# Moving GpSimd's projection sums and the deviations between the two steps of a pair

## The chip, the cores and the metric

The kernel runs on one core of a Trainium2 chip. The metric is the device time of one execution in microseconds (us). A core has five engines with a queue of instructions each: TensorE (PE in the profile, its weight loads PEld), VectorE (DVE), ScalarE (ACT), GpSimd (POOL) and SyncE (SP, which here only issues transfers). They wait for each other on semaphores.

## The reference

```
X = np.fft.rfft(x, axis=1)                 # x: 8 x 3136 x 256
y = np.fft.irfft(X * (filt_r + 1j*filt_i), n=3136, axis=1)
h = y.reshape(25088, 256) @ w_in           # 256 -> 1024
e = np.exp(h - max(h)); solu = h * e / (sum(e) + 1e-9)
ln = (solu - mean(solu)) / sqrt(var(solu) + 1e-6) * g_ln
out = ln @ w_out                           # 1024 -> 256
```

A filter along the sequence in the frequency domain, for each of 8 batch elements, and then a SoLU network with a layer norm on each of the 25088 tokens. All is float32.

## The kernel before, in words

The Fourier transforms are done as products with tables, in two stages, each with a passage through DRAM. The first element is transformed before the network starts; the transforms of the other seven are laid out by a hand-written plan (`PLAN`, and lists of jobs by step) beside the network for the elements before them.

The network takes 196 blocks of 128 tokens, two blocks to a pair. A pair is worked at by two calls of `step(k)`: the even step k = 2j and the odd one k = 2j + 1. There is no scheduler: every engine runs its instructions in the order in which `step` writes them (`tc.manual_schedule()`), so a line's place in `step` is its place in the queue of its engine. Both large products are done by a scheme of seven half-size products instead of eight; for it some sums of the inputs and weights are needed. In `step`, these things concern the change:

- `product(j, m)` (L715) are the seven products of the first matrix. Their input sums come from `pair_sums(j + 1)` on GpSimd (L704), at the start of the odd step.
- `exponential`, `normalize`, `square` and `turn` make solu of a block, the sum of squares (`var`), and a VectorE transpose into `turn`.
- `regroup(p, i)` (L790, its DMAs L799) fetches the two blocks of a pair out of the turned tile with eight DMAs of SP, into tiles `solu_t`. It stands in the even step of j for pair p = j - 3.
- `project_sums(p, step)` (L818) are GpSimd's four sums for the second matrix: step 0 makes `u1` and a difference that is written over a part of `solu_t`, step 1 makes `u2` and `u4`. All four are recorded at L702, inside the helper `sum_of`.
- `project(p, m)` (L834, matmuls at L844) are the seven products of the second matrix: 1, 2, 6 and 7 in the odd step, 5, 3 and 4 in the even step after it. Products 5, 6, 7 and 3 need the four sums.
- `deviations(p)` (L802) is done once for a group of two pairs: GpSimd makes `rs`, one over the standard deviation, with two small instructions (L806, L808), and SP stores it to DRAM (`rows`, L810). `regroup_deviations(g)` (L812) reloads it with four DMAs of SP in the order of the regrouped tokens (`rs_t`, L816).
- `keep_out` (ScalarE, L856) and `finish_out` (VectorE, L860) scale the projection by `rs_t`; `store_out` (SP, L868) writes it.
- For the transforms, GpSimd adds two quarters of the input (L260) before PE's products at L269, and issues the DMAs `t<-d` (`fetch_back`, L356), `d<-x` (L280), `d<-g` (L343) and `f<-f_dram` (L642). SP loads the input of these transforms (`x<-in_x_dram`, L245).

The jobs lists `stores[k]`, `products[k]` and `top[k]` run at the start of a step, `late[k]` and `loads[k]` at its end. `u2` and `u4` have one buffer each, the other sums and `solu_t` two.

Of the kernel before, what the change touches and what calls it, by code (L numbers as in the profile page):

```python
# [94 lines left out]
def kernel(  # L95
# [88 lines left out]
    class Spectrum:  # L184
# [114 lines left out]
        def product(self, i, out, lhsT, rhs):  # L299
            for v in range(self.units[i][1]):  # L300
                nc.tensor.matmul(out=out[:, v, :], lhsT=lhsT(v), rhs=rhs[:, v, :],  # L301
                                 start=True, stop=True)
# [398 lines left out]
    def sum_of(out, in0, in1, op):  # L701
        nc.gpsimd.tensor_tensor(out=out, in0=in0, in1=in1, op=op)  # L702

    def pair_sums(j):  # L704

        s14 = upool.tile([P, 2, P], FP32, name=f"s14_{j}", tag="s14")
        s23 = wk.tile([P, 2, P], FP32, name=f"s23_{j}", tag="s23")
        sums[j] = s1, s2, s3, s4 = s14[:, 0, :], s23[:, 0, :], s23[:, 1, :], s14[:, 1, :]
        a11, a12, a21, a22 = (tokens(2 * j + i, c) for i in range(2) for c in range(KD))
        sum_of(s1, a21, a22, ALU.add)  # L710
        sum_of(s2, s1, a11, ALU.subtract)
        sum_of(s3, a11, a21, ALU.subtract)
        sum_of(s4, a12, s2, ALU.subtract)
# [15 lines left out]
    def keep(j, k, i):  # L729

        if k not in hs:
            hs[k] = hpool.tile([P, DFF], FP32, name=f"h_{k}", tag=f"h{k % 2}")
        nc.scalar.copy(out=h_half(k, i), in_=ms[j, 0])  # L733
# [17 lines left out]
    def exponential(k):  # L751

        e = wk.tile([P, DFF], FP32, name="e", tag="e")
        esum = small.tile([P, 1], FP32, name="esum", tag="esum", bufs=2)
        nc.scalar.activation(out=e, in_=hs[k], func=AFT.Exp, bias=nmaxs.pop(k)[:, 1:2], scale=-1.0,  # L755
                             accum_out=esum)
        es[k] = e, esum
# [44 lines left out]
    def deviations(p):  # L802
        g, second = divmod(p, 2)
        if not second:
            rs = small.tile([P, 4], FP32, name=f"rs_{g}", tag="rs", bufs=2)
            nc.gpsimd.tensor_scalar(out=rs, in0=variances.pop(g), scalar1=1.0 / DFF, scalar2=EPS_LN,  # L806
                                    op0=ALU.mult, op1=ALU.add)
            nc.gpsimd.tensor_tensor(out=rs, in0=rs, in1=neg_half, op=ALU.pow)  # L808
            rs_rows[g] = rows = rs_dram.tile([P, 4], FP32, name=f"rows_{g}", tag="rows")
            nc.sync.dma_start(out=rows, in_=rs)  # L810

    def regroup_deviations(g):  # L812
        rows = rs_rows.pop(g).rearrange("(a p) b -> b p a", p=32)
        rss[g] = small.tile([P, 4], FP32, name=f"rs_t_{g}", tag="rs_t")
        for b in range(4):
            nc.sync.dma_start(out=rss[g][32 * b:32 * b + 32, :], in_=rows[b])  # L816

    def project_sums(p, step):  # L818

        (a11, a12), (a21, a22) = solu_ts[p, 0], solu_ts[p, 1]  # L820
        if step == 0:
            s1 = upool.tile([P, KF // 2, P], FP32, name=f"u1_{p}", tag="u1")
            sum_of(s1, a21, a22, ALU.add)
            sum_of(a21, a11, a21, ALU.subtract)
            solu_sums[p] = s1, None, a21, None
        else:
            s2 = spool.tile([P, KF // 2, P], FP32, name=f"u2_{p}", tag="u2")
            s4 = spool.tile([P, KF // 2, P], FP32, name=f"u4_{p}", tag="u4")
            s1, _, s3, _ = solu_sums[p]
            sum_of(s2, s1, a11, ALU.subtract)  # L830
            sum_of(s4, a12, s2, ALU.subtract)
            solu_sums[p] = s1, s2, s3, s4

    def project(p, m):  # L834

        bank = {1: 0, 6: 0, 5: 0, 3: 0, 2: 1, 7: 1, 4: 1}[m]
        if m in (1, 2):
            pos[p, bank] = ps_o.tile([P, DFF // 2], FP32, name=f"o{m}_{p}", tag=f"o{bank}")[:, 0:P]
        s1, s2, s3, s4 = solu_sums[p]
        lhs = {1: solu_ts[p, 0][0], 2: solu_ts[p, 0][1], 4: solu_ts[p, 1][1], 5: s1, 6: s2, 7: s3,  # L840
               3: s4}[m]
        w = w_out_sb[:, {1: 0, 2: 1, 3: 2, 5: 3, 6: 4, 7: 5, 4: 6}[m]]
        for f in range(KF // 2):
            nc.tensor.matmul(out=pos[p, bank], lhsT=lhs[:, f, :], rhs=w[:, f, :],  # L844
                             start=f == 0 and m in (1, 2, 7), stop=True, skip_group_check=True)
# [8 lines left out]
    def keep_out(p, i, to):  # L854
        rs = out_half(p, i, 0)[1]
        nc.scalar.activation(out=out_half(p, *to)[0], in_=pos[p, 0], func=AFT.Copy, scale=rs)  # L856
# [89 lines left out]
    pairs = blocks // 2  # L946

    def step(k):
        j, odd = divmod(k, 2)
        p = j - (LAG - 1) // 2 if odd else j - (LAG + 1) // 2  # L950
        if not 0 <= p < pairs:
            p = None
        hid, proj = k < blocks, p is not None
        for job in top[k] + stores[k] + products[k]:
            job()
        if odd and j + 1 < pairs:
            pair_sums(j + 1)
        if not odd:
            if hid:
                product(j, 1)  # L960
                keep(j, k, 0)
            if 2 <= k < blocks + 2:
                exponential(k - 2)
            if proj:
                project(p, 5)
                keep_out(p, 1, (0, 1))
            if hid:
                product(j, 2)
            if 3 <= k < blocks + 3:
                turn(k - 3)  # L970
            if hid:
                finish(j, k, 0, (k, 0), 1)
            if proj:
                finish_out(p, 1, 1, (0, 1), 1)
            for job in early[k]:
                job()
            if 3 <= k < blocks + 3:
                square(k - 3)
            if hid:
                product(j, 6)  # L980
                keep(j, k + 1, 0)
            if proj:
                project(p, 3)
                keep_out(p, 0, (0, 1))
                project(p, 4)
            for job in spectrum_loads[k]:
                job()
            if 0 <= j - 3 < pairs:
                regroup(j - 3, 0)
                regroup(j - 3, 1)  # L990
            if 0 <= j - 4 < pairs:
                project_sums(j - 4, 1)
            if 0 <= j - 3 < pairs:
                deviations(j - 3)
            if hid:
                product(j, 7)
            if 2 <= k < blocks + 2:
                normalize(k - 2)
            for job in second_parts[k] + middle[k] + first_parts[k]:
                job()  # L1000
            if proj:
                finish_out(p, 1, 0, (1, 0), 1)
                store_out(p)
        else:
            if hid:
                product(j, 5)
                keep(j, k - 1, 1)
                finish(j, k, 1, (k - 1, 1), 2)
            for job in early[k]:
                job()  # L1010
            if proj:
                project(p, 1)
                keep_out(p, 0, (0, 0))
                project(p, 2)
                finish_out(p, 0, 0, (0, 0), 1)
            if 2 <= k < blocks + 2:
                exponential(k - 2)
            if hid:
                product(j, 3)
                product(j, 4)  # L1020
            if 0 <= j - 3 < pairs:
                project_sums(j - 3, 0)
                if (j - 3) % 2 == 0:
                    regroup_deviations((j - 3) // 2)
            if proj:
                project(p, 6)
                project(p, 7)
            for job in second_parts[k] + middle[k]:
                job()
            if 3 <= k < blocks + 3:  # L1030
                turn(k - 3)
            if hid:
                finish(j, k - 1, 1, None, 0)
                finish(j, k, 0, (k, 0), 2)
            if 2 <= k < blocks + 2:
                normalize(k - 2)
            if proj:
                keep_out(p, 1, (1, 0))
            if 3 <= k < blocks + 3:
                square(k - 3)  # L1040
            for job in first_parts[k]:
                job()
        for job in late[k] + loads[k]:
            job()
        if k in (0, 1, 3, 4, 5, 6, 7):
            prepare_w_out(k - (k > 2))
# [37 lines left out]
```

## Time and profile before

| | |
|---|---|
| median of 3 runs | 1651.52 us (1638.6 to 1654.56) |
| the profiled execution | 1631.78 us, its span 1630.0 us, granted clock 0.986 |
| PE busy | 1551.7 us, 95% of the span |
| DVE busy | 1303.8 us, 80% |
| POOL busy | 1151.2 us, 71% |
| ACT busy | 903.5 us, 55% |
| POOL's first projection sum, 98 times | 1262 / 1276 / 2315 ns (least, median, most) |
| the eight regrouping DMAs of a pair | 128 KB each, issued by SP |

Busy time is a sum over the span; an engine that is idle beside a busy PE costs nothing by that. In the lines of waits the numbers are the total in us, the number of times, and the longest.

### The profile page before, as it was taken

How to read it: one execution, taken by the hardware profiler on the slowest of the kernel's cores; microseconds unless marked ns; L12 is line 12 of the kernel's file. 1: busy time of each engine (PE TensorE's matmuls, PEld its weight loads, DVE VectorE, ACT ScalarE, POOL GpSimd, SP SyncE). 2: the span in 40 equal slices, each digit the busy share in tenths (PEclk: the TensorE clock that was granted, in tenths of full speed). 3: DMA queues.
4: the chain of work that ended last, by engine and by line, in shares of the span. 5: the costliest groups of instructions: out<-in, count | busy, mean ns of one | idle time of the engine just before them, and what ended most of it. 6: DMA issues, size and time to landing. Idle time of an engine off the chain costs nothing. (4 is left out here: it accounts for less than half of the span.)

```text
span 1630.0 us, 36971 instructions
## 1 busy us (share of the span) xinstructions
PE 1551.7 (95%) x12710; PEld 1048.3 (64%) x12710; DVE 1303.8 (80%) x2630; ACT 903.5 (55%) x1772; POOL 1151.2 (71%) x1328
## 2 busy tenths in 40 slices
PE   5898899999999999999999999999999999999997
PEld 1353366666666676667766676666766777777766
DVE  1686788898888889987889789887989777777772
ACT  2135455656655665565556655566555655566662
POOL 4446886588676867697687967778476666677774
PEclk8999899999999999999999999999999999999999
DMA  9887878777887768866787678866786555444443
GB/s 266 251 274 242 237 212 241 210 216 191 198 239 221 198 182 257 230 190 180 188 250 203 172 194 219 235 185 170 203 223 160 127 130 128 104 109 104 110 109 101
DMA packets 377805, 312.13 MB, mean 191 GB/s; under 512 B 63322, under 2 KB 343395, under 8 KB 377619
## 3 DMA queue, kind: packets, MB, share of 16 engines
q1 hardware_dynamic: 306260, 169.81, 40.8%
q0 software_dynamic: 34464, 101.68, 21.2%
q10 hardware_dynamic: 36896, 38.28, 7.9%
q8 instruction: 103, 1.69, 0.5%
q14 instruction: 82, 0.67, 0.1%
HBM read 124.86 MB, written 81.50 MB: 127 GB/s over the span
## 5 line engine op out<-in xcount | busy, mean ns | idle before, releaser
L844 PEld LDWEIGHTS o<-w_out_sb,solu_t 128*128 128x128 f32 x3136 | 382.0, 192 | 50.0 <-issue 43.6
L723 PE MATMUL m<-w_in_sb,s 128*128 128x512 f32 x784 | 398.7, 609 | 10.5 <-ACT h L733 5.3
L844 PE MATMUL o<-w_out_sb,solu_t 128*128 128x128 f32 x3136 | 401.5, 276 | 3.2 <-DVE ot L860 2.8
L844 PEld LDWEIGHTS o<-w_out_sb,u 128*128 128x128 f32 x2352 | 307.9, 192 | 147.4 <-issue 104.6
L702 POOL TENSOR_TENSOR u<-solu_t 128x512 f32<-128x512 f32 x98 | 132.5, 1352 | 276.6 <-DMA solu_t<-turn 165.8
L844 PE MATMUL o<-w_out_sb,u 128*128 128x128 f32 x2352 | 312.1, 276 | 8.7 <-ACT ot L856 7.8
L723 PE MATMUL m<-w_in_sb,y 128*128 128x512 f32 x588 | 311.1, 613 | 5.4 <-DVE nmax L747 3.3
L733 ACT COPY h<-m 128x512 f32<-128x512 f32 x294 | 173.2, 589 | 240.5 <-PE m L723 201.8
L771 DVE SCALAR_TENSOR_TENSOR h<-e,rsum,h 128x1024 f32<-128x1024 f32 x196 | 294.8, 1504 | 6.9
L856 ACT ACTIVATE ot<-o,rs_t 128x128 f32<-128x128 f32 x392 | 144.0, 367 | 254.1 <-PE o L844 238.3
L779 ACT ACTIVATE h<-h,nmu 128x1024 f32<-128x1024 f32 x196 | 224.9, 1148 | 59.6 <-DVE turn L787 59.2
L747 DVE CUSTOM_DVE_ANT_0 h<-m,h 128x512 f32<-128x512 f32 x196 | 134.0, 684 | 148.2 <-ACT h L733 94.8
L787 DVE STREAM_TRANSPOSE turn<-h 128x1024 f32<-128x1024 f32 x196 | 243.1, 1240 | 3.2
L755 ACT ACTIVATE e<-h,nmax 128x1024 f32<-128x1024 f32 x196 | 225.2, 1149 | 6.5 <-DVE h L771 6.5
L702 POOL TENSOR_TENSOR u<-solu_t,u 128x512 f32<-128x512 f32 x98 | 147.8, 1508 | 79.2 <-PE o L844 74.2
L723 PEld LDWEIGHTS m<-w_in_sb,s 128*128 128x128 f32 x784 | 128.6, 192 | 100.0 <-issue 85.6
L723 PEld LDWEIGHTS m<-w_in_sb,y 128*128 128x128 f32 x588 | 96.9, 192 | 104.4 <-issue 52.2
L860 DVE SCALAR_TENSOR_TENSOR ot<-o,rs_t,ot 128x128 f32<-128x128 f32 x294 | 102.0, 347 | 76.0 <-ACT ot L856 57.1
L702 POOL TENSOR_TENSOR u<-u,solu_t 128x512 f32<-128x512 f32 x98 | 158.9, 1621 | 1.2
L702 POOL TENSOR_TENSOR solu_t<-solu_t,solu_t 128x512 f32<-128x512 f32 x98 | 142.4, 1453 | 7.7
L702 POOL TENSOR_TENSOR s<-y 128x128 f32<-128x128 f32 x196 | 103.4, 527 | 0.4
L372 PEld LDWEIGHTS py<-wb_t,t 50*64 50x64 f32 x3584 | 57.6, 134 | 43.2 <-issue 21.2
(114 smaller groups left out, 1963.8 us busy)
## 6 DMA issues: line engine op xcount, KB each, us to landing
solu_t<-turn SPq DMA_DIRECT2D x784, 128.0 KB
out_dram<-ot SPq DMA_DIRECT2D x196, 128.0 KB
t<-d POOLq DMA_DIRECT2D x112, 200.0 KB, 4.4
d<-x POOLq DMA_DIRECT2D x100, 200.0 KB, 5.5
f<-f_dram POOLq DMA_DIRECT2D x39, 512.0 KB, 7.9
d<-g POOLq DMA_DIRECT2D x39, 512.0 KB, 5.5
t<-d ACTq DMA_DIRECT2D x36, 512.0 KB
x<-in_x_dram SPq DMA_DIRECT2D x112, 98.0 KB
```

Of the source, the lines that this page charges most:

```text
L372: nc.tensor.matmul(out=views[g][64 * h:64 * h + 64, cb, i, :], lhsT=t4[rows, i, c0:c0 + 64], rhs=wb_t[rows, 0:N1], start=True, stop=True)
L702: nc.gpsimd.tensor_tensor(out=out, in0=in0, in1=in1, op=op)
L723: nc.tensor.matmul(out=ms[j, bank], lhsT=lhsT, rhs=w_in_sb[:, w, :], start=m in (1, 2, 7), stop=True, skip_group_check=True)
L733: nc.scalar.copy(out=h_half(k, i), in_=ms[j, 0])
L747: nc.vector.tensor_tensor_reduce(out=h_half(k, i), in0=ms[j, bank], in1=h_half(*kept), scale=1.0, scalar=sofar, op0=ALU.add, op1=ALU.min, ...
L755: nc.scalar.activation(out=e, in_=hs[k], func=AFT.Exp, bias=nmaxs.pop(k)[:, 1:2], scale=-1.0, accum_out=esum)
L771: nc.vector.scalar_tensor_tensor(out=solu, in0=e, scalar=rsum, in1=solu, op0=ALU.mult, op1=ALU.mult, accum_out=nmu)
L779: nc.scalar.activation(out=solu, in_=solu, func=AFT.Square, bias=nmu, scale=-float(DFF), accum_out=variances[g][:, i:i + 1])
L787: nc.vector.transpose(out=turns[g][:, :, i, :], in_=solus[k].rearrange("p (f j) -> p f j", j=32))
L844: nc.tensor.matmul(out=pos[p, bank], lhsT=lhs[:, f, :], rhs=w[:, f, :], start=f == 0 and m in (1, 2, 7), stop=True, skip_group_check=True)
L856: nc.scalar.activation(out=out_half(p, *to)[0], in_=pos[p, 0], func=AFT.Copy, scale=rs)
L860: nc.vector.scalar_tensor_tensor(out=ot, in0=pos[p, bank], scalar=rs, in1=out_half(p, *kept)[0], op0=ALU.mult, op1=ALU.add)
```

## The change

All four sums of a pair now stand in the even step: the first two, which stood in the odd step before, at its very start, the other two where they were. The deviations' two GpSimd instructions and their store move from the even step into the odd one, after the pair sums, to where the first two sums had been. The reload of the deviations moves from the odd step to the start of the next even step. No instruction is added or removed, and no size changes.

```
         hid, proj = k < blocks, p is not None
+        if not odd and 0 <= j - 4 < pairs:
+            if j % 2 == 0:
+                regroup_deviations((j - 4) // 2)
+            project_sums(j - 4, 0)
         for job in top[k] + stores[k] + products[k]:
             job()
...
             if 0 <= j - 4 < pairs:
                 project_sums(j - 4, 1)
-            if 0 <= j - 3 < pairs:
-                deviations(j - 3)
             if hid:
                 product(j, 7)
...
             if 0 <= j - 3 < pairs:
-                project_sums(j - 3, 0)
-                if (j - 3) % 2 == 0:
-                    regroup_deviations((j - 3) // 2)
+                deviations(j - 3)
             if proj:
                 project(p, 6)
```

More of the change, by code (lines that the diff above doesn't have):

```diff
@@ L953, in step @@
         hid, proj = k < blocks, p is not None
+        if not odd and 0 <= j - 4 < pairs:
+            if j % 2 == 0:
+                regroup_deviations((j - 4) // 2)
+            project_sums(j - 4, 0)
         for job in top[k] + stores[k] + products[k]:
@@ L992, in step @@
                 project_sums(j - 4, 1)
-            if 0 <= j - 3 < pairs:
-                deviations(j - 3)
             if hid:
@@ L1021, in step @@
             if 0 <= j - 3 < pairs:
-                project_sums(j - 3, 0)
-                if (j - 3) % 2 == 0:
-                    regroup_deviations((j - 3) // 2)
+                deviations(j - 3)
             if proj:
```

## The prediction

> **What bounds the kernel now.** I read the page's busy shares first, then the windows by stage, the waits of PE and POOL, the timeline of one pair, and the chain at the end.
>
> ```profile
> PE 1551.7 (95%) x12710; PEld 1048.3 (64%) x12710; DVE 1303.8 (80%) x2630; ACT 903.5 (55%) x1772; POOL 1151.2 (71%) x1328
> 800.00:1000.00 200.00, 197.15 (x1770) 135.31 (x1769) 174.62 (x346) 117.80 (x233) 151.89 (x175) 0.99 0.77 210
> 1400.00:1500.00 100.00, 99.86 (x571) 72.05 (x570) 77.68 (x173) 61.68 (x122) 73.22 (x73) 1.00 0.43 108
> 1600.00:1630.00 30.00, 19.13 (x161) 18.12 (x159) 3.15 (x9) 4.41 (x12) 12.38 (x11) 0.93 0.38 98
> PE pa L269 <- POOL x L260: 7.2, 5, 2.0
> POOL u L702 <- DMA solu_t<-turn: 142.3, 31, 9.1
> ```
>
> The first line is the page; the next three are windows (length, then busy time of PE, PEld, DVE, ACT, POOL, then clock, DMA share, GB/s). PE is the bound: in the stage where Fourier work and the network run together (about 250 to 1250 us) it is 98 to 99% busy, from 1250 to 1580 us over 99%; only the last 30 us are loose. The last two lines are waits between 250 and 1250 us (total, times, longest). POOL waits 142.3 us for the regrouped tile and PE hardly notices; what PE loses to POOL is 7.2 us, before the forward transform, on L260, the sum of quarters. So a gain must come out of a few microseconds there or at the end, however large POOL's wait is.
>
> One pair on POOL, then PE, SP and ACT at the same place (start, duration, idle and releaser in brackets):
>
> ```profile
> 810.51 1.85 POOL L702 TENSOR_TENSOR u<-solu_t 128x512 f32<-128x512 f32 x1 [6.78 <-DMA solu_t<-turn]
> 812.44 1.27 POOL L702 TENSOR_TENSOR solu_t<-solu_t,solu_t 128x512 f32<-128x512 f32 x1
> 813.65 1.09 POOL L356 DMA_DIRECT2D t<-d  x2
> 818.93 0.51 POOL L806 TENSOR_SCALAR rs<-var 128x4 f32<-128x4 f32 x1
> 819.52 1.04 POOL L808 TENSOR_TENSOR rs<-rs,neg_half 128x4 f32<-128x4 f32 x1
> 821.38 1.28 POOL L260 TENSOR_TENSOR x<-x 113x512 f32<-113x512 f32 x1
> 822.71 0.65 PE L269 MATMUL pa<-x,wq_t 49*64 49x512 f32 x2 [2.00 <-POOL x L260]
> 820.59 0.36 SPq L810 DMA_DIRECT2D rows<-rs  x1
> 822.73 2.45 SPq L245 DMA_DIRECT2D x<-in_x_dram  x4
> 825.77 4.20 SPq L816 DMA_DIRECT2D rs_t<-rows  x4
> 830.12 7.85 SPq L799 DMA_DIRECT2D solu_t<-turn  x8
> 835.75 0.37 ACT L856 ACTIVATE ot<-o,rs_t 128x128 f32<-128x128 f32 x1 [0.30 <-PE o L844]
> ```
>
> The reader is to see that the two deviation instructions stand just ahead of the sum of quarters that PE waits for, and that ACT's first use of the reloaded deviations comes ten microseconds after the reload began. The end of the chain of waits:
>
> ```profile
> 1603.30 2.09 DMA rows<-rs
> 1606.76 2.98 DMA rs_t<-rows
> 1609.92 0.38 ACT ot L856
> 1610.43 2.93 PE o L844 x24
> ```
>
> Here nothing covers the deviations' trip through DRAM: store, reload, scaling and PE follow each other, and the end waits for them.
>
> [...]POOL stood 6.78 us before its first sum with its loads queued behind. [...]SP's reloads waited 25.8 us in all for the store of rows, so SP's place in its queue matters. [...] the same first sum takes 1.262 to 2.315 us, so moved sums may meet other VectorE work.
>
> **The change, part by part.** No instruction is added or removed, and the order on PE, ACT and DVE stays. Only POOL and SP are reordered.
>
> *The first two sums (u1, and the one written back into solu_t).* On POOL they now stand behind the odd step's tail, the loads t<-d (L356, 1.09 us for two), and in front of the same stores and second sums as before. So the wait for the regrouped tile is still in POOL's queue; "a step later" moves it past 1.09 us of issues at most. Where the tile is late, the issues are hidden in the wait; where it is ready, the sums start 1.1 us later. Cover: product 6 of the projection started 4 to 5 us after the third sum (u2), which it needs, in most pairs of this stage, later still after 1250 us. In six pairs of it the cover was 1.3 us or less (pair 39: the third sum ends at 817.5, product 6 starts at 817.7), but before each of these POOL had waited over 5 us for the tile, and there the move costs nothing. Earlier t<-d traffic (two DMAs of 200 KB) can slow the regrouping in flight: nothing to 2 us in such a pair; a loss of 1 us in a few of them is taken in the range, nothing in the sum. Another meeting with VectorE costs or saves up to 1 us (2.3 against 1.3), beside a cover of 4: nothing.
>
> *The deviations on POOL.* 818.93 to 820.53, 1.6 us in 49 of 98 pairs, move from before to after the sum of quarters and the pair sums. Both come 1.6 us earlier in these pairs. Each PE wait on L260 that the timeline shows in the stage follows a deviation, as here. Five waits of 7.2 us, the longest 2.0; with the weight load that precedes them some 8.5 us. At most 1.6 us comes back of each, and not all are that long: gain 7 us, bounds 4 and 9. What is late next there is PE's own queue.
>
> *SP.* The store of rows moves behind the stores of the output and the x loads, the four reloads to the start of the next even step, ahead of eight regroupings as before. Output and x loads lose a wait (SP waited 23.6 us for rs in all); PE shows no wait for either: gain nothing to 2, taken 0. The store now needs POOL's pair sums, then 1.6 us. Worked at the pair above: rs ends at about 825.4, where the pair sums ended, 4.8 us later than before; store lands 2.1 us later, 827.6; the reloads, 1.8 us when SP is free and 4.2 us as here, end at 829.4 to 831.9; 2.7 us to landing (1607.2 to 1609.9 at the end) gives 832.1 to 834.6. ACT needs them at 835.75, so 1.1 to 3.6 us remain. For the other groups of this stage I took the end of the pair sums and of the first projection product from the timeline: between them lie 7.1 us in the shortest, about 10 in the middle. The trip needs 6.7, up to 9.5 under load. A dozen groups would then wait up to 2.4 us, 16 us of ACT in all, if every trip were loaded. Before, ACT waited 4.2 us in four cases in this stage, and once 4.2 us at the end. PE has three products (2.6 us) before product 6 adds into the bank that the scaling reads, so short waits pass it by; as an estimate half reaches it. I take a quarter of the loaded case, 4 us of ACT, 2 us of PE; bounds 0 and 8.
>
> The regroupings of the second pair of a group wait for the reloads: 0 to 2.4 us later than before. POOL then waits that much longer, but u2 has its 4 to 5 us: nothing.
>
> *The end.* POOL's order is the same there. On SP the last store of rows follows two output stores (1.3 us) that stood behind it: 1604.4 against 1603.30. Nothing hides it: plus 1.1 us, bounds 0.5 and 2.
>
> Sum: -7 + 2 + 1.1 = about -4 us. The profiled execution was 1631.78 us (span 1630.0), so 1628 in its terms; the median of the three runs is 1651.52, and its runs lie 1638.6 to 1654.56. I put the difference on the median: 1647.5.
>
> **The rivals.**
> *The deviations arrive late (slower).* Mechanism: ACT stands before its first scaling (L856) for rs_t, and exponentials and copies of h queue behind it. For it: four output scalings in this stage already met late reloads; SP has one queue and the x loads lie ahead of the store. Against: ACT is 55% busy, and the 2.6 us of products above. It begins to cost at a trip of 7 us, at 9.5 us PE loses 8 us. With a trip of 11 us in all groups the shortfalls add up to about 40 us of ACT, half on PE, 20: less 4 of the net gain, +16, giving 1667.5. It decides from 11 us.
> *POOL's lateness ran through more than L260 shows (faster).* Earlier pair sums, t<-d and x loads would also take waits now listed under DVE and ACT (PE's listed waits in the stage are 20 us in all). All of these and none of the losses: -18, giving 1633.5. Against: most are waits for ACT and DVE, whose order is kept.
> *Nothing moves.* PE is at 98 to 99% and the few waits return in another pair: 0 to +1.1, 1652.
>
> **How the numbers follow.** Forecast, -9 to -1 us: 0.5. Nothing moves, within 3 us: 0.22. Late deviations: 0.17, of which 0.12 over 1% (16.5 us is 1%, about what a measurement can tell from no change). Faster chain: 0.11, of which 0.08 over 1%. So faster 0.08, same 0.80, slower 0.12. Range: the forecast with its bounds, and the spread of the runs, gives 1635 to 1656; reaching towards the rivals 1634 to 1662.
>
> **What would show it.** Right: PE's wait on L260 in the stage falls from 7.2 to under 2 us; POOL's wait for solu_t<-turn stays above 100 us, now behind t<-d; the second sums start within 2 us of where they stood against PE; ACT's wait on rs_t stays under 15 us; the last rows store starts about 1 us later against the last regrouping. Wrong: ACT waits of tens of microseconds for rs_t, PE waiting on POOL's u sums, or the stage from 1250 to 1580 us below 99% on PE.

## The result, and the profile after

The changed kernel takes 1704.31 us (median of four runs, 1696.06 to 1709.93). The kernel before, run on the same chip, takes 1645.86 us (1638.6 to 1654.56). The ratio is 1.0349, with a 95% interval of 1.0274 to 1.0424: slower by 58 us where the forecast was 4 us faster, and outside the range. The profiled execution took 1696.06 us with a span of 1694.2, so 64 us more span than the one before.

First the busy time of each engine in the changed kernel; then the chain of waits that ended last, by engine, of the kernel before; then the same of the changed kernel, by engine and by line:

```profile
PE 1567.6 (93%) x12710; PEld 1060.9 (63%) x12710; DVE 1290.8 (76%) x2630; ACT 904.8 (53%) x1772; POOL 1141.4 (67%) x1328
```

```profile
PE 23%; DVE 1%; SPq 0%; issue 0%; DMA 0%; ACT 0%; POOL 0%; DVEq 0%; ACTq 0%
```

```profile
PE 46%; DMA 18%; POOL 4%; DVE 3%; SPq 3%; issue 3%; ACT 1%; ACTq 0%; POOLq 0%; DVEq 0%
PE o L844 22%; PE m L723 19%; DMA solu_t<-turn 5%; DMA rows<-rs 4%; DMA rs_t<-rows 3%; DMA out_dram<-ot 2%; PE py L372 2%; DMA t<-d 2%; DMA x<-in_x_dram 1%; PE pa L269 1%; SPq L799 1%; PE pc L301 1%; POOL u L702 1%; POOL s L702 1%; DMA de<-de_tbl 1%
```

PE has fallen from 95 to 93%. In the changed kernel transfers have 18% of the chain, and the store and reload of the deviations (rows, rs_t) stand among its lines by name; before, they had 0%. The two chains are not of one length (the shares sum to about a quarter of the span before and over three quarters after), so the 18% names the lines and does not measure the loss.

The windows by stage (length, busy PE, PEld, DVE, ACT, POOL, then clock, DMA share, GB/s), first of the kernel before for the stage as a whole, then four of after:

```profile
250.00:1250.00 1000.00, 980.72 (x9031) 671.44 (x9028) 868.75 (x1716) 585.61 (x1159) 740.78 (x865) 1.00 0.76 206
```

```profile
250.00:1250.00 1000.00, 943.26 (x8507) 646.27 (x8509) 804.08 (x1619) 554.26 (x1096) 697.38 (x829) 0.98 0.73 197
800.00:1000.00 200.00, 189.78 (x1639) 130.72 (x1637) 158.79 (x321) 110.67 (x218) 143.82 (x170) 0.97 0.72 197
1460.00:1560.00 100.00, 100.00 (x574) 72.58 (x573) 78.17 (x173) 62.35 (x124) 71.80 (x74) 1.00 0.43 108
1660.00:1690.00 30.00, 20.11 (x152) 19.14 (x152) 3.16 (x9) 4.13 (x12) 12.61 (x12) 0.89 0.35 91
```

Two things are lost in the long stage: PE stands more, and its clock is 0.97 to 0.98 instead of 0.99 to 1.00, so that 943 us of busy PE do less than they look. The light stage is as full as before. Read by the start of a pair's first product, the changed kernel is 13.7 us late at pair 16 (384 us before), 59.8 at pair 76 (1306 us) and 59.1 at pair 96 (1561 us), and 64 at the end. So 14 us are lost by 384 us, about 46 between 384 and 1306, nothing in the light stage, and 5 at the end.

The waits of after between 250 and 1300 us (total, times, longest), SP's among them:

```profile
POOL u L702 <- DMA solu_t<-turn: 147.3, 28, 10.2
...
ACT ot L856 <- DMA rs_t<-rows: 62.1, 19, 8.9
...
PE o L844 <- ACT ot L856: 23.2, 12, 5.1
...
ACT h L733 <- DMA rs_t<-rows: 17.7, 4, 7.0
...
DVE diff L254 <- DMA x<-in_x_dram: 15.2, 8, 4.4
...
SPq L816 <- DMA rows<-rs: 157.1, 32, 8.0
```

The same waits of before, in the same stretch:

```profile
ACT ot L856 <- DMA rs_t<-rows: 4.3, 4, 1.8
...
PE o L844 <- ACT ot L856: 0.7, 1, 0.7
...
DVE diff L254 <- DMA x<-in_x_dram: 5.7, 5, 2.3
...
SPq L816 <- DMA rows<-rs: 23.0, 16, 5.1
```

All listed waits of PE in this stretch have grown from 18.7 to 58.9 us; 23.2 us of them are for the scaling. PE's wait on the sum of quarters (L269 on L260) has no line any more. Two waits have grown together: ScalarE stands for the deviations, and SP stands at their reload, up to 8 us in each of 32 groups.

One of the later groups, on SP, then ACT and PE:

```profile
854.39 1.32 SPq L868 DMA_DIRECT2D out_dram<-ot  x2
855.95 2.19 SPq L245 DMA_DIRECT2D x<-in_x_dram  x4
858.23 0.53 SPq L810 DMA_DIRECT2D rows<-rs  x1
866.03 2.09 SPq L816 DMA_DIRECT2D rs_t<-rows  x4
868.22 8.46 SPq L799 DMA_DIRECT2D solu_t<-turn  x8
876.78 1.31 SPq L868 DMA_DIRECT2D out_dram<-ot  x2
878.28 2.23 SPq L245 DMA_DIRECT2D x<-in_x_dram  x4
...
875.54 0.37 ACT L856 ACTIVATE ot<-o,rs_t 128x128 f32<-128x128 f32 x1 [6.91 <-DMA solu_t<-turn]
...
876.05 2.05 PE L844 MATMUL o<-w_out_sb,u 128*128 128x128 f32 x8 [4.54 <-ACT ot L856]
```

GpSimd ended rs at 857.50. SP issued the store at 858.23, behind two output stores and four x loads, and could issue the reload only at 866.03: 7.8 us, in which SP did nothing. The reloads were issued by 868.12, and ScalarE's scaling ran at 875.54, 7.4 us later. (The trace names solu_t as what ended ScalarE's wait; the scaling reads rs_t, not solu_t.) So the trip took 18.0 us from the end of rs to the scaling (13.1 in the middle of the late groups), ScalarE stood 6.9, and PE, after its three covering products, 4.5. Behind SP's hold the regrouping of the next pair, the output stores and the x loads went out late as well.

There is a second place where ScalarE stands. ScalarE issues loads of its own (ACTq), and some of them wait for the reload, on SP, ScalarE and PE:

```profile
472.12 3.00 SPq L816 DMA_DIRECT2D rs_t<-rows  x4
...
477.40 0.37 ACTq L683 DMA_DIRECT2D de<-de_tbl  x1
477.81 0.59 ACT L733 COPY h<-m 128x512 f32<-128x512 f32 x1 [6.99 <-DMA rs_t<-rows]
...
478.54 1.68 PE L723 MATMUL m<-w_in_sb,s 128*128 128x512 f32 x2 [3.73 <-ACT h L733]
```

The load of a table (L683) and the copy of h behind it read nothing of rs_t. In the trace the load waits for the semaphore that the first reload, issued at 472.12, was to raise, and goes out at 477.40, when that reload has landed (477.38). Most of the line `ACT h L733 <- DMA rs_t<-rows` above is such stops. No run tested them by themselves.

What PE's stop costs beyond itself is seen in the windows of after around it:

```profile
866.00:871.00 5.00, 5.00 (x27) 3.24 (x25) 3.29 (x7) 0.59 (x1) 4.12 (x6) 1.00 0.74 224
...
876.00:878.00 2.00, 1.95 (x9) 1.98 (x10) 1.97 (x4) 1.03 (x2) 0.00 (x0) 0.50 0.70 178
...
880.00:882.00 2.00, 2.00 (x20) 1.08 (x20) 1.93 (x6) 0.84 (x3) 1.10 (x1) 0.58 0.57 179
882.00:884.00 2.00, 2.00 (x15) 0.96 (x8) 1.51 (x3) 2.00 (x5) 0.79 (x1) 1.00 0.22 78
```

The granted clock is 1.00 ahead of the stop, 0.50 when PE goes on, and 1.00 again only from about 882: five to six microseconds at about half speed, 2.8 us lost on top of 4.5. This group is not alone: in this stage of after PE stands longer than 2 us nine times (2.4 to 5.1 us, four of them for ScalarE's scaling, three for its copies of h or t, one each for VectorE and GpSimd), and each time 1.6 to 3.0 us of clock are lost in the 6 us behind it. The stretches at 0.50 last 3.4 or 6.8 us there. Before, it never stands longer than 2.0 us there, but both stops of 2.0 us, on the sum of quarters, were followed by 3.4 us at 0.50 as well, 1.7 us lost each. One of them is the stop that the prediction shows at 822.71; this window of before lies behind it:

```profile
824.00:827.00 3.00, 3.00 (x10) 1.97 (x10) 1.03 (x1) 2.65 (x6) 2.84 (x6) 0.50 0.87 236
```

Not every such stop has a lower clock behind it: before, two of 2.4 us (from 1586.7 and 1608.0 us) were followed by 6 us at 1.00, and so was one of 2.6 us in after (from 201.4 us). What decides it is not shown.

The end of the chain of after:

```profile
1664.59 5.04 DMA rows<-rs
1669.65 0.30 SPq L816
...
1682.27 0.38 ACT ot L856
```

The last store takes 5.04 us where it took 2.09, and after the reload the chain runs over the regrouping and the output stores instead of going straight to the scaling. (This is the scaling of the last pair, 1682.27; the chain gives an output store as what it waited for.)

From the trace one can add up what PE loses over the whole run: the time between two matmuls where it is over 0.3 us, and, outside of these, the clock that was not granted (one less the share, times the length of each clock record). Both are worked out from the records of the profiled executions (the runs are those of the next section), and their change accounts for the change of the span within 7 us:

| kernel | PE stands | clock lost while it runs | sum less before | span less before |
|---|---|---|---|---|
| before | 60.4 | 18.9 | | |
| after | 109.7 | 35.7 | +66.1 | +64.2 |
| deviations only | 98.4 | 31.1 | +50.1 | +56.5 |
| older scale | 96.9 | 35.2 | +52.8 | +51.6 |
| older scale, reload last | 70.9 | 21.0 | +12.6 | +8.8 |
| reload by GpSimd | 129.4 | 40.2 | +90.2 | +90.5 |
| reload last | 409.7 | 129.4 | +459.8 | +454.9 |

### The profile page after: what moved, and what is told of

It reads as the page before. It is cut to its first block, busy times and chain, and to the rows that moved or that the text cites. A ratio compares the mean times of both kernels' runs of the same rounds, so it can differ in the third digit from the quotient of the medians.

```text
span 1694.2 us, 36993 instructions
## 1 busy us (share of the span) xinstructions
PE 1567.6 (93%) x12710; PEld 1060.9 (63%) x12710; DVE 1290.8 (76%) x2630; ACT 904.8 (53%) x1772; POOL 1141.4 (67%) x1328
## 4 chain that ended last, share of the span: by engine, by line
PE 46%; DMA 18%; POOL 4%; DVE 3%; SPq 3%; issue 3%; ACT 1%; ACTq 0%; POOLq 0%; DVEq 0%
PE o L844 22%; PE m L723 19%; DMA solu_t<-turn 5%; DMA rows<-rs 4%; DMA rs_t<-rows 3%; DMA out_dram<-ot 2%; PE py L372 2%; DMA t<-d 2%; DMA x<-in_x_dram 1%; PE pa L269 1%; SPq L799 1%; PE pc L301 1%; POOL u L702 1%; POOL s L702 1%; DMA de<-de_tbl 1%
## 5 line engine op out<-in xcount | busy, mean ns | idle before, releaser
L844 PEld LDWEIGHTS o<-w_out_sb,u 128*128 128x128 f32 x2352 | 312.3, 195 | 184.5 <-issue 134.4
L844 PEld LDWEIGHTS o<-w_out_sb,solu_t 128*128 128x128 f32 x3136 | 389.1, 195 | 47.5 <-issue 43.0
L844 PE MATMUL o<-w_out_sb,solu_t 128*128 128x128 f32 x3136 | 407.3, 279 | 2.4 <-DVE ot L860 2.3
L844 PE MATMUL o<-w_out_sb,u 128*128 128x128 f32 x2352 | 319.6, 280 | 39.8 <-ACT ot L856 34.6
L733 ACT COPY h<-m 128x512 f32<-128x512 f32 x294 | 173.3, 589 | 252.8 <-PE m L723 218.8
L771 DVE SCALAR_TENSOR_TENSOR h<-e,rsum,h 128x1024 f32<-128x1024 f32 x196 | 297.3, 1517 | 6.9
L702 POOL TENSOR_TENSOR solu_t<-solu_t,solu_t 128x512 f32<-128x512 f32 x98 | 153.5, 1566 | 7.7
L702 POOL TENSOR_TENSOR u<-u,solu_t 128x512 f32<-128x512 f32 x98 | 147.3, 1503 | 0.9
L702 POOL TENSOR_TENSOR s<-y 128x128 f32<-128x128 f32 x196 | 95.5, 487 | 0.4
```

Source lines behind the costliest of these rows:

```text
L771: nc.vector.scalar_tensor_tensor(out=solu, in0=e, scalar=rsum, in1=solu, op0=ALU.mult, op1=ALU.mult, accum_out=nmu)
```

## The experiments

The first theory was that ScalarE's wait for late deviations is the loss (A in the expectations, where a letter is used). Its rivals were that the moved sums of GpSimd are (B), or half and half (C). That SP's hold at the reload is a cause came in after the third run. All ratios are to the kernel before, run on the same chip, with 95% intervals. "Lateness" is the time from the end of a group's first projection product to its scaling, summed over the groups of 250 to 1300 us where it is over half a microsecond: 11.0 us before, 91.7 after.

**The sums alone.** Of the change only the move of the first two sums; deviations and reload as before.

```
+        if not odd and 0 <= j - 4 < pairs:
+            project_sums(j - 4, 0)
...
-                project_sums(j - 3, 0)
```

> Only the sums move: all four in the even step as in the changed kernel; deviations, their store and their reload stay where they were before. Theory A (the loss is ScalarE's wait for the reloaded deviations, whose trip through DRAM now starts some 4 us nearer to its use): the time is that of before, 1646 us, within 8; ScalarE's wait for rs_t stays below 15 us in all, against 70 in the changed kernel. Rival B (the sums' move does it: the t<-d loads, issued earlier, slow the regrouping, and the sums then hold up the projection): the time is near 1704. Rival C (half and half): about 1675.

Measured: 1634.16 us against 1640.37, ratio 0.9965 [0.9947, 0.9982]; lateness 12.8 us, PE's wait on L260 4.3. The sums' move costs nothing; it brings about 6 us.

**The deviations alone.** The other part: the deviations in the odd step, right behind the pair sums and so ahead of the first two sums, their reload first in the even step, the sums in their steps as before.

```
+        if not odd and 0 <= j - 4 < pairs and j % 2 == 0:
+            regroup_deviations((j - 4) // 2)
...
-            if 0 <= j - 3 < pairs:
-                deviations(j - 3)
...
             if 0 <= j - 3 < pairs:
+                deviations(j - 3)
                 project_sums(j - 3, 0)
-                if (j - 3) % 2 == 0:
-                    regroup_deviations((j - 3) // 2)
```

> Only the deviations move: rs in the odd step after the pair sums, its store there, the reload at the start of the next even step; the sums stay in their two steps. Theory A: all of the loss is here, 1695 to 1710 us, ScalarE waiting 60 us or more for rs_t. Rival B: 1640 to 1650 us, since nothing in front of the projection has moved. Rival C: about 1675.

Measured: 1687.5 us, 1.0281 [1.0228, 1.0333]; lateness 87.4, SP's wait for rows in the stage 134.8 us. The loss belongs to this part. The changed kernel's 1.0349 stands beside it with an overlapping interval. PE's longest listed waits here are for the copies of h (24.8 us in 8 cases) ahead of those for the scaling (12.0), and the longest of all is at a stop of ScalarE in front of loads of its own, on ScalarE and PE:

```profile
479.13 0.37 ACTq L683 DMA_DIRECT2D de<-de_tbl  x1
479.53 0.58 ACT L733 COPY h<-m 128x512 f32<-128x512 f32 x1 [13.07 <-DMA rs_t<-rows]
...
480.26 2.05 PE L723 MATMUL m<-w_in_sb,s 128*128 128x512 f32 x2 [9.81 <-ACT h L733]
```

**An older scale.** The changed kernel, but the scaling reads the deviations of the group before. Store, reload and SP's order stay as in the change; only what ScalarE waits for is long there.

```
-        return ..., rss[p // 2][...]
+        return ..., rss[max(p // 2 - 1, 0)][...]
```

> The changed kernel, but the projection is scaled with the reloaded deviations of the group before (the first group with its own): the same instructions and transfers, and nobody waits for the reload of the same group. Theory A: the loss goes, 1640 to 1650 us; if the 7 us that were to be gained before the forward transform are real, it is below before, near 1640. Rival B: stays at 1695 to 1710.

Measured: 1691.6 us, 1.0322 [1.0257, 1.0387]. The waits between 250 and 1300 us:

```profile
DVE diff L254 <- DMA x<-in_x_dram: 48.5, 19, 5.4
...
PE m L723 <- DVE nmax L747: 26.5, 14, 3.6
...
ACT ot L856 <- DMA rs_t<-rows: 0.6, 2, 0.3
...
SPq L816 <- DMA rows<-rs: 157.2, 32, 8.4
```

ScalarE's wait ahead of the scaling is gone, and the loss stays. So the first theory fell: without that wait the changed kernel loses about as much. SP's hold is the same 157 us, and now VectorE stands 48.5 us for the x loads behind it; the maximum (nmax) that PE waits for stands right behind that in VectorE's queue. ScalarE's stops at its own loads are still there (11.6 us ahead of copies of h for rs_t). In place of the first theory came another (D): two channels lie side by side, ScalarE's wait for rs_t and SP's hold, and PE pays the later of the two. That PE pays just the later one is an argument that no run shows in this form.

**The store by GpSimd.** The changed kernel, with the store of rows issued by GpSimd behind rs itself, ahead of SP's output stores and x loads.

```
-            nc.sync.dma_start(out=rows, in_=rs)
+            nc.gpsimd.dma_start(out=rows, in_=rs)
```

> The changed kernel with the small store of rows issued by GpSimd itself, right after it has made rs, instead of by SP behind the output stores and the loads of x. If the store is slow because its packets lie behind those in SP's rings (in the changed kernel the reload starts 5 us after the store, against 2 us where nothing is ahead of it), SP's reload starts 2 to 3 us earlier, ScalarE's wait for rs_t falls to about half and the time to 1670 to 1685. If the store is slow because the transfers are busy as a whole, or the reload itself is the longer part, the time stays within 8 us of 1704.

Measured: 1672.0 us, 1.0201 [1.0134, 1.0267]; lateness 51.8 us, SP's wait for rows still 167.3. A sooner store takes some of the loss away, not the hold. In part the hold only moved: in the changed kernel SP also stood 28.9 us at the store, for rs, and the two together went from 186.0 to 167.3 us. The store itself was not quicker on GpSimd's queue: from issue to landing 5.2 us in the middle of the groups between 250 and 1300 us, against 5.4 on SP's, by the semaphores in the traces. So it is as slow without the output stores and x loads ahead of it in its queue.

**An older scale and the reload last.** The older scale again, and the four reloads behind the regroupings, output stores and x loads, at the end of the even step.

```
-            if j % 2 == 0:
-                regroup_deviations((j - 4) // 2)
...
+        if not odd and 0 <= j - 4 < pairs and j % 2 == 0:
+            regroup_deviations((j - 4) // 2)
```

> The kernel with the scale of the group before, and its reload moved from the start of the even step to its end, behind the regrouping, the output stores and the loads of x on SP; nobody waits for it soon, and SP meets the store of rows when it has long landed. Theory D (two channels side by side, each enough for the loss: ScalarE waits for rs_t, and SP, held at the reload by the landing of rows, hands out the regrouping and the loads of x some 4 us late, on which VectorE and GpSimd wait in order): with both cut the time falls to that of the sums-only kernel or below, 1625 to 1640 us against 1640 of before; VectorE's wait for x, 48 us with the older scale alone, falls below 15. Rival E (the older place of rs on GpSimd, or more traffic of t<-d, costs by itself): it stays above 1670.

Measured: 1640.8 us against 1638.53, 1.0007 [0.999, 1.0023]. The waits in the stage:

```profile
DVE diff L254 <- DMA x<-in_x_dram: 19.1, 13, 5.5
...
PE m L723 <- DVE nmax L747: 5.9, 6, 3.2
...
SPq L816 <- DMA out_dram<-ot: 35.0, 30, 3.4
```

SP has no wait for rows left (at its new place the reload waits 35.0 us for output stores instead), and the loss is gone with it. Between this kernel and the first one with the older scale only the place of the reload in SP's queue differs: that alone is worth 3%. VectorE's wait for x is less than half of the 48.5 us there, though above what was expected, and the time just above too.

**The sums and the reload's place.** The sums alone, as above, and the reload first in the even step, with the deviations left where they were before.

```
         if not odd and 0 <= j - 4 < pairs:
+            if j % 2 == 0:
+                regroup_deviations((j - 4) // 2)
             project_sums(j - 4, 0)
...
-                if (j - 3) % 2 == 0:
-                    regroup_deviations((j - 3) // 2)
```

> The sums and the reload move as in the changed kernel; rs and its store stay in the even step. On SP the reload then stands where it stood in nearly all groups (directly ahead of the regrouping), and the store of rows is again ahead of the output stores and the loads of x. Theory D: SP doesn't wait at the reload, so the time is that of the sums-only kernel, 1630 to 1642 us: the loss belongs to rs and its store, not to the reload's place. Rival F (the reload's new place is a cost of its own): 1660 or more.

Measured: 1634.01 us, 0.9964 [0.9941, 0.9988]; lateness 12.8, SP's wait for rows 27.9. The reload's place at the start of the even step is harmless as long as the store is early; SP stands in the changed kernel because the store has moved up close to the reload.

**The sums, with the store by GpSimd**, and **the same with the deviations ahead of the last two sums**:

```
-            nc.sync.dma_start(out=rows, in_=rs)
+            nc.gpsimd.dma_start(out=rows, in_=rs)
...
+            if 0 <= j - 3 < pairs:
+                deviations(j - 3)
             if 0 <= j - 4 < pairs:
                 project_sums(j - 4, 1)
-            if 0 <= j - 3 < pairs:
-                deviations(j - 3)
```

> The sums-only kernel, with the store of rows issued by GpSimd right after rs. SP loses one issue and its wait for rs in 49 groups, GpSimd gains an issue of some 0.6 us in each. If the trip of the deviations still costs something in the sums-only kernel (ScalarE late by over 1 us in 6 groups, 13 us in all), 3 to 8 us below it, 1626 to 1631; if not, within 3 us of 1634.

Measured: 1642.17 us, 1.0031 [1.0011, 1.0051]: worse than the sums alone. SP's wait for rows was 69.0 us; with the store on SP it was 29.2, and 11.4 more at the store for rs. So SP stood longer. This was not expected.

> As the kernel before it in this list, with rs between the first two and the last two sums of the even step, so that it and its store start some 3 us earlier and the last two sums 1.6 us later in every second pair. By theory D an earlier start of the trip can only help until no reload is late: 0 to 5 us below that kernel. Rival G: the last two sums, 1.6 us later, hold up the projection where their cover is short, or GpSimd waits for the squares: 0 to 10 us above it.

Measured: 1636.18 us, 0.9983 [0.9965, 1.0001], 6 us below the one before it; from the end of rs to the end of the first projection product 17.1 us instead of 14.1, SP's wait for rows 7.2. So rs earlier takes SP's wait away. It doesn't repair all of what the other store lost: the next run is this kernel with the store back on SP, where SP waits longer for rows (25.9) and the time is still lower by 0.5%. SP's wait is therefore not what a store by GpSimd costs here; what it is stays open.

**The deviations ahead of the last two sums, store on SP**: with the sums' move, and alone on the kernel before. The edit is the lower half of the last diff.

> The first two sums at the start of the even step, the deviations in the even step as in the kernel before but ahead of the last two sums, the store of rows by SP. If the trip of the deviations is what this part of the kernel has to cover (two channels: ScalarE waits for rs_t, SP is held at the reload), then rs ends some 2.5 us earlier than with the sums' move alone, ScalarE's waits for rs_t fall from 9.8 us to under 4, SP's wait for rows stays under 20 us, and the time is 1629 to 1634. If the last two sums, now 1.6 us later in every other pair, are what product 6 and those after it need, PE gains waits on POOL's sums and the time is 1636 to 1645.

Measured: 1625.6 us against 1637.26, 0.9934 [0.991, 0.9958], below what was expected. ScalarE's wait for rs_t in the scaling did not fall under 4 us (8.8), nor SP's for rows under 20 (25.9), so the gain is not shown to be the trip's.

> The kernel before with one edit: in the even step the deviations stand ahead of the last two sums instead of behind them; the first two sums stay in the odd step. It tells what the best time so far, 0.9934 of the kernel before, is made of. If the earlier deviations give their part alone (their stop in front of the sum of quarters is gone by 1.6 us either way, rs ends 2.5 us earlier), the ratio is 0.996 to 0.998, and PE's waits on the sum of quarters and SP's wait for rows stay below 8 and 25 us. If the gain comes only with the sums' move, 0.999 to 1.002. If the later second sums cost, above 1.002.

Measured: 1634.87 us against 1640.15, 0.9957 [0.9935, 0.9979]; SP's wait for rows 25.4 us, just over what was expected. PE's wait on the sum of quarters in the stage, first with the deviations' move alone, then with both moves:

```profile
PE pa L269 <- POOL x L260: 0.5, 2, 0.3
```

```profile
PE pa L269 <- POOL x L260: 1.3, 3, 0.6
```

It was 7.2 us before and 4.3 with the sums' move alone. Each edit gives about 0.4%, and together they give 0.66%: nearly the sum. What fell in the traces is PE's wait for GpSimd. That this makes the gain is argued and not shown: the profiled execution of the run with the deviations' move alone was the slowest of its eleven (1640.0 us), and PE's waits for the copies of h are longer in it (8.8 us against 2.2). The version with both is faster than the kernel before and the changed one.

**The reload by GpSimd.** The changed kernel, with the four reloads taken out of SP's queue and put in GpSimd's, in front of its first sums.

```
-            nc.sync.dma_start(out=rss[g][32 * b:32 * b + 32, :], in_=rows[b])
+            nc.gpsimd.dma_start(out=rss[g][32 * b:32 * b + 32, :], in_=rows[b])
```

> The changed kernel, with the four reload DMAs issued by GpSimd instead of SP, at the same place of the step, ahead of its first sums, where it waits for the regrouped tile anyway. Only SP's hold goes: its wait for rows at the reload falls from 157 us to nothing, and regroupings and x loads are handed out as before. The reload itself is as late as in the changed kernel, so ScalarE's waits for rs_t stay at 60 to 110 us. If both channels cost alone, as the run with the older scale says of the other one, 1675 to 1700. If SP's hold carries the loss and ScalarE's wait is hidden on PE, 1640 to 1655. GpSimd then stands at the reload in SP's place, and its sums after it come later: a third channel, which would show as PE or SP waiting on POOL's sums.

Measured: 1728.76 us, 1.0549 [1.0504, 1.0594], above both expectations. The waits in the stage:

```profile
POOL rs_t L816 <- DMA rows<-rs: 198.2, 31, 9.5
...
PE o L844 <- POOL u L702: 47.0, 21, 5.0
```

The hold went with the DMAs: GpSimd now stands 198 us, its sums come late, and PE stands 47 us for them. The third channel named at the end of the expectation took SP's place, and costs more. ScalarE's lateness was still 69 us, of which PE's waits for the scaling show only 3.6; but PE stood for the sums beside it. So this run does not show what ScalarE's wait costs alone.

**The reload last, with the group's own deviations.** That is what the last run was for: the changed kernel with the reload at the end of the even step, as in the run at 1.0007, but with the right group's deviations.

> The changed kernel with its reload at the end of the even step, behind the regroupings, output stores and x loads, and with this group's own deviations in the scaling. With the older scale this place of the reload gave the time of the kernel before (1.0007), so what it loses here is ScalarE's channel alone: SP should not be held for rows (below 10 us), while every reload lands some 8 us later than in the changed kernel. If ScalarE's wait for rs_t costs by itself, its lateness between 250 and 1300 us grows from 92 to 200 to 350 us, PE's waits on ScalarE's scaling with it, and the time is 1700 to 1850. If PE's products beside it hide the wait, the time is 1640 to 1660 in spite of that lateness.

Measured: 2084.16 us against 1633.63, 1.2732 [1.2666, 1.2798]. SP's wait for rows at the reload has no line. The waits over the whole run, and in the timeline PE at one group:

```profile
ACT ot L856 <- DMA rs_t<-rows: 476.8, 48, 15.3
PE o L844 <- ACT ot L856: 375.4, 55, 13.0
```

```profile
1015.24 2.05 PE L844 MATMUL o<-w_out_sb,u 128*128 128x128 f32 x8 [10.42 <-ACT ot L856]
```

The lateness of all groups of the run adds up to 473 us, and the time to 451 more than before. Between 250 and 1300 us the lateness is 281 us, as expected; the time is far above, because the light stage is late too and because hardly any of it is hidden. Against the run at 1.0007 only the group whose deviations are read differs. So ScalarE's channel alone can cost, at nearly one to one: PE stands for about three quarters of it, and the halved clock afterwards makes up the rest (the table above: 349 us of standing, 110 of clock).

## Why the prediction was wrong

**PE's wait on the sum of quarters: right.** It went from 7.2 us to nothing (under 2 was expected). In the changed kernel the gain drowns in the loss. The run with the deviations alone ahead of the last sums fits it: 0.5 us of wait left, 5 to 7 us less time (by the medians, and by the ratio 0.9957). Two of these waits, of 2.0 us, also cost 1.7 us of clock each, which the forecast didn't count.

**The first two sums behind the odd step's tail: right.** They cost nothing; alone they gave 6 us where nothing was counted. Of these 3 are the shorter wait on L260; the rest was not traced. The two risks that the prediction weighs there can be seen in the trace of before. The first sums that start while VectorE runs L771 take 1.27 to 2.32 us (18 of 98), the others 1.26 to 1.29. And in the stage a regrouping DMA landed 2.9 us after its issue, in the middle of 58, where nothing moved on GpSimd's DMA queue, and 6.3 us in the middle of 352 where over 60 GB/s did; that this traffic is the cause is not shown.

**The deviations' trip: wrong, and the first of two steps that failed.** The cover, from the end of rs to the end of the first projection product, was about right: 7.1 us in the shortest and about 10 in the middle were taken, 5.8 and 9.4 measured. The trip was taken at 6.7 us with numbers from the idle end of the run, and up to 9.5 under load (its own lines, 825.4 to 834.6, give 9.2). Between 250 and 1300 us it measured 13.1 us in the middle of the 25 groups of 32 that came over 1 us late (8.2 to 19.6). The mis-sized term is the store above all: 2.1 us were taken from its issue to the reload's, 5.4 measured in the middle of these groups (2.8 to 8.4). From the last reload's issue to the scaling 2.7 were taken and 3.7 measured; the 7.8 and 7.4 of the group shown are near the long end. The sign of being wrong that the prediction names, ScalarE waiting tens of microseconds for rs_t, came: 62.1.

The trace of before had part of the answer: between 250 and 1300 us the store took 3.5 us in the middle, up to 8.9, and 5.1 in the very pair that the prediction shows. The other part is its new place in time: in the light stage, in the middle of eleven groups each, it took 1.9 us before and 4.5 after. Why is not shown. With GpSimd issuing it in the changed kernel it took 4.2, so SP's queue alone doesn't explain it.

**How much of ScalarE's lateness reaches PE: too small for long waits.** Half was taken, on the strength of three covering products, and of a lateness of 16 us only a quarter. The lateness was 91.7 us. The cover of 2.6 us holds for short waits; the groups here are late by up to 8.6 us. PE's waits for the scaling are 23.2 us in the changed kernel; in the run with the reload last nearly all comes through.

**SP's hold: wrong, and the second step that failed.** "The regroupings of the second pair of a group wait for the reloads: 0 to 2.4 us later ... nothing", and output and x loads "lose a wait". SP's wait for rows in the stage rose from 23.0 to 157.1 us. With the scale made independent of the reload the loss is still 3.2%, and all of it goes when the reload is put behind the other transfers. The hold lasts as long as the store, so it was sized by the same 2.1 us; and the sentence looked at the regroupings behind the reload but not at the x loads behind those, for which VectorE and PE wait. ScalarE's own loads, which stand until a reload has landed, had no term; the 3.2% are the hold together with these. In the light stage there are no x loads, and SP's hold, 54.3 us in 13 cases between 1300 and 1640 us, costs nothing.

**The clock: no term at all.** A stall of PE was priced at its length. A quarter of the loss, 16.8 of 66 us, is clock that is not granted, most of it behind the nine stops of 2.4 us and more.

**The end: right in place, small in size.** 1.1 us were taken for the store's later start. The last 70 us grew by 5: by the chain, the store also takes 3 us longer, behind two output stores, and the way from the reload to the last scaling leads over the regrouping and the output stores.

**The rival "the deviations arrive late"** had the mechanism, and its condition was met: it decides from a trip of 11 us, and the trip was 13. Its price of 16 us was too low first of all because its 40 us of ScalarE's waits were 92; it also halved PE's share, and left out SP's hold and the clock. (In its sum the 2 us that the forecast had already counted for late deviations come in twice; 14 is what its terms give.) How the 64 us divide between the two channels stays open: each can cost alone (3.2% without ScalarE's wait ahead of the scaling; nearly one to one without SP's hold), they lie side by side in the same groups, no run had ScalarE's wait alone at the size that it has in the changed kernel, and none took away its stops at its own loads alone.

**The light stage: right.** PE stays at 100% there. The trip is 10.6 us in the middle, and no scaling is late.

## What to carry to other kernels

When a small store and its reload are moved closer together, measure the trip where the kernel is loaded (here 13 to 18 us, against 6.7 taken from the idle end), and ask of the issuing queue not only who waits for the reload but what else stands behind it. Taking one of two parallel waits away can leave the loss as it was (1.0322 here against 1.0349), and moving the waiting instruction to another engine moved the hold with it (157.1 us on SP, 198.2 on GpSimd). A stop of PE of some microseconds cost about a third more than its length in four of the five slow kernels of the table, and 45% more in the one with the older scale.

## What the runs showed that was not expected

- A 2 KB store that took 2.09 us in the idle end took 7.8 us in the group shown, behind two output stores and four x loads on the same queue, and 5.04 in the end behind output stores alone. On GpSimd's queue it was as slow (5.2 against 5.4 in the middle).
- With the sums moved, GpSimd issuing that store in SP's stead left SP standing longer (69.0 us against 29.2 and 11.4 at the store). With rs ahead of the last two sums SP stood shorter (7.2 against 25.9), and the time was longer all the same.
- ScalarE stood up to 13.1 us, and PE up to 9.8, while loads that ScalarE issues waited for the landing of the store or the reload of the deviations, which they don't read.
- PE's clock fell to 0.50 behind stops as short as 2.0 us (in the kernel before), though not behind two of 2.4 us in the same kernel, and took five to six microseconds to come back in the group shown.
- Standing and lost clock together account for the change of span within 7 us in all six kernels of the table.
